# Retention feeding a routed expert layer: the first list made a little later, two guessed loads made one, and sixteen zero scatters made three

## The chip, the cores and the metric

The kernel runs on one core of a Trainium2 chip. The metric is device microseconds from the start to the end of one execution. The core has five instruction streams: TensorE (PE in the profile; PEld is its weight load), VectorE (DVE), ScalarE (ACT), GpSimd (POOL) and SyncE (SP). SP here issues the plain loads, and POOL issues the indirect DMAs, which write rows to places given by a list of row numbers.

## The reference

Two stages follow each other. The first is a retention layer (a linear attention with a decaying state) over 4 sequences, 8 heads, 768 steps and 64 features. The second sends each of the 3072 resulting rows to one of 8 experts, a two-layer network of 512 by 1024 by 512.

```python
for t in range(S):
    state = gamma[None, :, None, None] * state + np.einsum('bhd,bhe->bhde', k[:, :, t], v[:, :, t])
    y[:, :, t] = scale * np.einsum('bhd,bhde->bhe', q[:, :, t], state)
...
logits = x @ w_gate + modality_bias[modality_id]
e_idx = np.argmax(logits, axis=1)
...
for e in range(E):
    mask = e_idx == e
    h = np.maximum(x[mask] @ w1[e], 0.0)
    out[mask] = gate_w[mask, None] * (h @ w2[e])
```

`gate_w` is the softmax probability of the chosen expert. All inputs are float32.

## The kernel before, in words

**Retention.** The 3072 rows are 24 blocks of 128, numbered n. For each block the kernel loads keys and queries (`kq`) and keys and values by token (`kv`), 512 KB each. The first nine blocks go in a "whole" form (scores L277, state L299, output L313 and L319), the later ones in "quarters" (all at L267). A block's output is copied transposed (`yT`, L325), multiplied with a matrix that also holds the gate (L379), and becomes rows of x (`xs`, DVE L387 and ACT L401) and logits (`lh`).

**Routing.** Three blocks are a group. For a group, `route_a` finds each row's expert and adds to the counts `cnt`; `ranks` turns the counts into the fill of 96 candidate slots of 256 rows (matmul `pc` L619, then a key per slot); `route_b` gives each row its place (matmul `rk` L456 to L463); `gates` fills the gate into the rows; `scatter` (L485, POOL) writes the group's three blocks of rows to their places in `x_dram`. After groups 1, 2, 4, 5 and 6 `early_a` and `early_b` make a short list of two full slots (matmuls `pk` L641 and `pt` L692, list `lst` L696). A list is two slots, so ten jobs "e"; a final list brings two jobs "s" and some remainders of 32 rows. After group 0 a guess is made: the expert with most rows so far (`lst_g`). Its weights are loaded before the first list is known.

**A job** is 256 rows through one expert. SP reads slot and expert from the list into registers (TENSOR_LOAD L958), loads two row tiles `xg` of 128 rows (L810), then the expert's w1 and w2 as four tiles `raw1` and four `raw2` of 512 KB (L778, or L780 where the load is skipped if the expert is the one already there). `cut` splits a weight tile in two parts, `hi` by ACT (L784) and `lo` by DVE (L786). The rows are transposed by PE (`xp_e` L829) and split too (`xTh` by ACT L798, `xTl` by DVE L799). Then `first_slot` (L844) makes h with three products for each pair of parts, `second` (L859) makes o, ACT scales it (L871) and POOL scatters it to the output (L872).

**Order.** PE, ACT, DVE and SP work in the order in which the program writes their instructions; POOL's order is found by a scheduler. The program advances in steps. At each step one function of the list `todo` is taken (`tick`), and retention goes on to its next `yield`. Before the first job there are only retention and routing; once the first list is there, the row loads and weight loads of the first job are issued, `AHEAD` steps are counted down while retention goes on, the first two `cut`s of w1 and the transposes (`flip_x`) fall in steps on the way, and then the job begins. In a job of some 14 steps, every third step takes one step of retention.

**Zero rows.** The last slots of each expert are not full. After the final list `pad_a`, `pad_b` and `pad_c` compute the places behind each expert's last row, and 16 indirect DMAs (two for each expert, 128 rows of 2056 bytes each, `pad_c` L545) write zero rows there. Places that need no zeros get a number out of bounds. The row loads of the last three jobs wait for these scatters.

Of the kernel before, what the change touches and what calls it, by code (L numbers as in the profile page):

```python
# [7 lines left out]
F32 = mybir.dt.float32  # L8
F32R = mybir.dt.float32r
BF16 = mybir.dt.bfloat16  # L10
# [24 lines left out]
NTAIL = 2  # L35
NUNIT = 144

AHEAD = 6

WHOLE = 9  # L40
EMPTY = 2 * NCAND
# [12 lines left out]
def kernel(  # L54
# [23 lines left out]
    def bank(name):  # L78
        return ps.tile([P, 512], F32, tag="bank", name=name)
# [10 lines left out]
    lent = {("kq", n): f"hi2{n - 4}" for n in range(4, 8)}  # L90
    lent.update({("kv", n): f"lo2{n - 3}" for n in range(3, 7)})

    def room(kind, n, bufs):
        shape, name = [P, 2, DM], f"{kind}_{n}"
        if (kind, n) in lent:
            return me.tile(shape, F32, tag=lent[kind, n], name=name)
        return ld.tile(shape, F32, tag=kind, name=name, bufs=bufs)

    def load_kq(n, parts=1):
# [71 lines left out]
    def zero_rows(nm):  # L171
        zer = wk.tile([P, ROW], F32, tag="xs", name=nm, bufs=6)
        nc.gpsimd.memset(zer, 0.0)
        nc.gpsimd.memset(zer.bitcast(I32)[:, DM : DM + 1], NT)
        return zer
# [318 lines left out]
        scattered.setdefault(gr, []).append(getattr(ins, "ins", ins))  # L494


    def pad_a():
        tot = bank("tot")[:, :NE]
        nc.tensor.matmul(tot, ones, cnt[NGRP], start=True, stop=True)
        shape = [P, NE, 2]  # L500
        at = cp.tile(shape, F32, name="pad_at")
        row = cp.tile([P, 2], F32, name="pad_row")
        nc.gpsimd.iota(
            row, [[P, 2]], base=0, channel_multiplier=1, allow_small_or_imprecise_dtypes=True
        )

        num = cp.tile([P, NE], F32, name="pad_num")
        nc.vector.tensor_copy(num, tot)
        numi = cp.tile([P, NE], I32, name="pad_numi")
        nc.vector.tensor_copy(numi, num)  # L510
        lasti = cp.tile([P, NE], I32, name="pad_lasti")
        nc.vector.tensor_scalar(lasti, numi, SLOT - 1, None, op0=ALU.bitwise_and)
        last = cp.tile([P, NE], F32, name="pad_last")
        nc.vector.tensor_copy(last, lasti)
        none = cp.tile([P, NE], F32, name="pad_none")
        nc.vector.tensor_scalar(none, last, 0.0, float(SLOT), op0=ALU.is_equal, op1=ALU.mult)
        nc.vector.tensor_tensor(last, last, none, op=ALU.add)
        nc.vector.tensor_tensor(
            at, last.unsqueeze(2).to_broadcast(shape), row.unsqueeze(1).to_broadcast(shape),
            op=ALU.add,  # L520
        )
        over = cp.tile(shape, F32, name="pad_over")
        nc.vector.tensor_scalar(
            over, at, float(SLOT), float(2 * ZROW), op0=ALU.is_ge, op1=ALU.mult
        )
        nc.vector.scalar_tensor_tensor(
            num, iota3[:, 0], float(NT), num, op0=ALU.mult, op1=ALU.add
        )
        mid["pad"] = (row, num, over)

    def pad_b():
        row, num, over = mid.pop("pad")
        shape = [P, NE, 2]
        nc.vector.tensor_tensor(
            over, over, num.unsqueeze(2).to_broadcast(shape), op=ALU.add
        )
        mid["zero"] = zero_rows("zer2")
        pad = mid["pad"] = cp.tile(shape, I32, name="pad_i")
        nc.vector.tensor_tensor(
            pad, over, row.unsqueeze(1).to_broadcast(shape), op=ALU.add  # L540
        )

    def pad_c(e):
        for h in range(2):
            ins = nc.gpsimd.indirect_dma_start(  # L545
                out=x_dram[:, :],
                out_offset=bass.IndirectOffsetOnAxis(ap=mid["pad"][:, e, h : h + 1], axis=0),
                in_=mid["zero"],
                in_offset=None,
                bounds_check=ZROW - 1,  # L550
                oob_is_err=False,
            )
            disjoint(ins, "x_rows")


    off_c = cnd[:, 0:1]
# [245 lines left out]
    def load_rows(tag, at, full=None):  # L802
        xg = []
        assert sum(len(scattered.get(gr, [])) for gr in range(NGRP if full is None else full + 1)) == (
            NN if full is None else (full + 1) * GRP
        )
        for hh, r in enumerate(at):
            t = me.tile([P, ROW], F32, tag=f"xg{hh}", name=f"xg{hh}_{tag}", bufs=2)
            r = r() if callable(r) else r
            ins = nc.sync.dma_start(t, x_dram[bass.ds(r * P, P), :])  # L810
# [358 lines left out]
    def everything():  # L1169
# [171 lines left out]
```

## Time and profile before

| | us |
|---|---|
| runs of the kernel before | 431.11, 432.29, 435.65 |
| their median | 432.29 |
| the profiled execution, its own time | 429.24 |
| its span, as the trace has it | 427.2 |
| PE busy in the span | 403.8 (95%) |
| DVE, ACT, POOL busy | 247.5, 207.7, 103.1 |

The span runs from the first to the last instruction that the trace shows; 2.04 us of the profiled execution's time lie around it. The profiled execution is 3.05 us faster than the median. "PEclk" or the granted clock is the share of TensorE's full clock that it was allowed in a stretch. A row of a window view gives the window, its length, and the busy time and count of PE, PEld, DVE, ACT and POOL, then PE's clock, the DMA share and GB/s. A row of the timeline gives start, duration, engine, line, operation, what it writes from what, shapes and count, and in square brackets how long the engine was idle before it and what ended that. A row of the wait view gives who waited for what, the total, how often, and the longest.

### The profile page before, as it was taken

The numbers are of one execution on the slowest core, as the hardware profiler recorded it, in microseconds if no ns is written. First come the engines' busy times: TensorE is split into PE (matmuls) and PEld (weight loads), VectorE is DVE, ScalarE is ACT, GpSimd is POOL, SyncE is SP. The second block draws the span as 40 slices with busy tenths as digits, with TensorE's granted clock in tenths as the row PEclk, the third lists the DMA queues.
The fourth block names the chain that finished last, engine by engine and source line by source line (L and its number), as shares of the span: only waits on it lengthen the run. The fifth ranks groups of instructions, "written<-read, shape, count | busy, mean of one in ns | idle before, by whom it ended". The sixth has DMA issues, their size and how long they took to land.

```text
span 427.2 us, 12026 instructions
## 1 busy us (share of the span) xinstructions
PE 403.8 (95%) x4596; PEld 352.8 (83%) x4596; DVE 247.5 (58%) x590; ACT 207.7 (49%) x420; POOL 103.1 (24%) x130
## 2 busy tenths in 40 slices
PE   4998869999999999999999999999999999999994
PEld 3887749988968977988898998989899898967863
DVE  1775537855726674756754765768565574634700
ACT  1233346754627444655645564655465563636511
POOL 2424401233033114112510210130486100002001
PEclk9998979999999999999999999999999999999998
DMA  8999748877787955137760213762253898999001
GB/s 289 398 405 371 270 143 263 297 265 252 255 294 261 302 209 187 50 125 254 241 224 28 94 58 123 269 201 76 67 174 130 310 337 280 383 387 345 27 0 45
DMA packets 30891, 92.79 MB, mean 217 GB/s; under 512 B 5550, under 2 KB 5678, under 8 KB 30832
## 3 DMA queue, kind: packets, MB, share of 16 engines
q1 hardware_dynamic: 25360, 77.83, 52.8%
q0 software_dynamic: 5184, 13.67, 8.6%
q8 instruction: 37, 0.61, 0.6%
q10 hardware_dynamic: 288, 0.50, 0.3%
q14 instruction: 22, 0.18, 0.1%
HBM read 94.84 MB, written 17.21 MB: 262 GB/s over the span
## 4 chain that ended last, share of the span: by engine, by line
PE 54%; issue 17%; DMA 5%; DVE 3%; POOL 3%; ACT 2%; POOLq 1%; SPq 0%; ACTq 0%
PE o_e L859 20%; PE h_e L844 20%; PE x L379 4%; PE st L267 3%; PE sc L267 3%; PE y L267 2%; DVE lo_e L786 2%; PE xp_e L829 2%; ACT hi_e L784 1%; DMA kv<-in_qkv_dram 1%; POOL out_dram L872 1%; POOL x_dram L545 1%; DMA x_dram<-zer,pad_i 1%; DMA xg_e<-x_dram 1%; DMA wa_u<-in_w_dram 1%
## 5 line engine op out<-in xcount | busy, mean ns | idle before, releaser
L786 DVE TENSOR_TENSOR lo_e<-raw,hi_e 128x1024 fp32r<-128x1024 f32 x80 | 99.8, 1248 | 83.9 <-ACT hi_e L784 75.9
L844 PE MATMUL h_e<-xTh,hi_e 128*128 128x256 f32 x320 | 91.8, 287 | 0.0
L844 PE MATMUL h_e<-xTl,hi_e 128*128 128x256 f32 x320 | 90.3, 282 | 0.0
L844 PE MATMUL h_e<-xTh,lo_e 128*128 128x256 f32 x320 | 90.3, 282 | 0.0
L784 ACT CAST hi_e<-raw 128x1024 fp32r<-128x1024 f32 x80 | 83.7, 1047 | 3.9 <-DMA raw<-in_w_dram 3.9
L859 PE MATMUL o_e<-hi_e,hTh 128*128 128x512 f32 x160 | 66.3, 414 | 0.0
L859 PE MATMUL o_e<-lo_e,hTh 128*128 128x512 f32 x160 | 63.1, 395 | 0.0
L859 PE MATMUL o_e<-hi_e,hTl 128*128 128x512 f32 x160 | 63.1, 394 | 0.0
L844 PEld LDWEIGHTS h_e<-xTh,hi_e 128*128 128x128 f32 x320 | 60.7, 190 | 0.7
L844 PEld LDWEIGHTS h_e<-xTh,lo_e 128*128 128x128 f32 x320 | 60.6, 190 | 0.3
L844 PEld LDWEIGHTS h_e<-xTl,hi_e 128*128 128x128 f32 x320 | 60.7, 190 | 0.0
L1032 POOL TENSOR_TENSOR vd<-kv,cst 128x512 f32<-128x512 f32 x24 | 27.2, 1133 | 96.7 <-PE y L267 38.7
L793 ACT ACTIVATE hTh<-h_e 128x256 fp32r<-128x256 f32 x80 | 30.7, 386 | 34.0 <-PE h_e L844 29.9
L872 POOL DMA_INDIRECT out_dram<-o_e,xg_e x20 | 20.6, 1032 | 110.2 <-ACT o_e L871 90.4
L401 ACT ACTIVATE xs<-x,cst 128x64 f32<-128x64 f32 x96 | 22.2, 314 | 43.7 <-DVE lh L387 25.1
L794 DVE SCALAR_TENSOR_TENSOR hTl<-h_e,hTh 128x256 fp32r<-128x256 f32 x80 | 33.1, 419 | 16.5 <-ACT hTh L793 14.8
L485 POOL DMA_INDIRECT x_dram<-xs,pos x24 | 26.9, 1119 | 44.9 <-DVE a L212 17.2
L859 PEld LDWEIGHTS o_e<-lo_e,hTh 128*128 128x128 f32 x160 | 30.1, 188 | 7.1
L859 PEld LDWEIGHTS o_e<-hi_e,hTh 128*128 128x128 f32 x160 | 30.1, 188 | 6.1
L859 PEld LDWEIGHTS o_e<-hi_e,hTl 128*128 128x128 f32 x160 | 30.2, 189 | 5.5
L871 ACT ACTIVATE o_e<-o_e,xg_e 128x512 f32<-128x512 f32 x20 | 13.8, 690 | 40.8 <-issue 23.9
L379 PE MATMUL x<-wgt,yT 128*128 128x144 f32 x192 | 30.7, 304 | 1.8 <-issue 1.8
(193 smaller groups left out, 677.8 us busy)
## 6 DMA issues: line engine op xcount, KB each, us to landing
raw<-in_w_dram SPq DMA_DIRECT2D x104, 512.0 KB
kv<-in_qkv_dram SPq DMA_DIRECT2D x24, 512.0 KB
kq<-in_qkv_dram SPq DMA_DIRECT2D x23, 512.0 KB
xg_e<-x_dram SPq DMA_DIRECT2D x20, 257.0 KB
wa_u<-in_w_dram SPq DMA_DIRECT2D x8, 512.0 KB
wb_u<-in_w_dram SPq DMA_DIRECT2D x16, 256.0 KB
xg_s<-x_dram SPq DMA_DIRECT2D x4, 257.0 KB
x_dram<-xs,pos POOLq DMA_INDIRECT x24
```

The costliest lines, as they stand in the source:

```text
L267: nc.tensor.matmul(out_, l, r, start=start, stop=True, skip_group_check=True)
L379: nc.tensor.matmul(px[:, g], yT[:, 2 * u + g], wgt[:, 2 * u + g], start=(g == 0), stop=(g == 1), skip_group_check=True,)
L401: nc.scalar.activation(x[:, i], px[:, i // 2, rows(i % 2)], AF.Copy, scale=gain[:, c, 4 * u + i : 4 * u + i + 1],)
L485: ins = nc.gpsimd.indirect_dma_start(out=x_dram[:, :], out_offset=bass.IndirectOffsetOnAxis(ap=pos[:, i : i + 1], axis=0), in_=xs, in_offs ...
L784: nc.scalar.copy(hi, raws[m][i])
L786: nc.vector.tensor_tensor(lo, raws[m][i], hi.bitcast(F32), op=ALU.subtract)
L793: nc.scalar.activation(hi, src, AF.Relu)
L794: nc.vector.scalar_tensor_tensor(lo, src, 0.0, hi.bitcast(F32), op0=ALU.max, op1=ALU.subtract)
L844: nc.tensor.matmul(ph, s["w1"][f // 2][wi][:, o : o + P], s["xT"][kc // 2][a][:, kc % 2, :], start=(n == 0), stop=(n == 3 * KC - 1),)
L859: nc.tensor.matmul(po, hT[f][a][:, hh * P : (hh + 1) * P], s["w2"][f // 2][wi][:, (f % 2) * DM : (f % 2 + 1) * DM], start=(n == 0), stop=( ...
L872: ins = nc.gpsimd.indirect_dma_start(out=out[:, :], out_offset=bass.IndirectOffsetOnAxis(ap=xg.bitcast(I32)[:, DM : DM + 1], axis=0), in_= ...
L1032: ins = nc.gpsimd.tensor_tensor(vds[n], vv, by[:, n % NCH].unsqueeze(2).to_broadcast([P, H, D]), op=ALU.mult)
```

## The change

1. **The guess.** Only the guessed expert's w1 is loaded ahead of the first list. The first job's w2 is loaded without condition once the list is there. `AHEAD` goes from 6 to 4 and the cuts and the flip are renumbered.
2. **The first list.** In group 1, gates, places and the scatters of the rows (`first_b`) come ahead of the candidate sizes; the list (`d`) is made two ticks later than before. Both row registers are loaded before both row loads. In group 4 a step of waiting is put in, so everything from there on in that group is a step later.
3. **The zero scatters.** The four rotating `kq` tiles become parts of one tile `four`, which after the last `kq` is set to zero by POOL and serves as source. Places are computed for runs of 8 rows (16,448 bytes for one row number) and single rows: two indirect DMAs write runs (experts 0 to 3 and 4 to 7), one writes single rows. `pad_a` (DVE) now comes before the three small matmuls of the new `pad_m`, and `pad_b` has 17 DVE operations.

The diff, cut to its core:

```diff
-AHEAD = 6
+RUN = 8
+AHEAD = 4
...
+    four = ld.tile([P, max(4 * QW, RUN * ROW)], F32, name="four", bufs=1)
+    fours = [four[:, i * QW : (i + 1) * QW] for i in range(4)]
+    free = [i for i in range(NN) if ("kq", i) not in lent]
...
+        if kind == "kq":
+            return fours[free.index(n) % 4].rearrange("p (a b) -> p a b", a=2)
...
     def pad_a():
-        tot = bank("tot")[:, :NE]
-        nc.tensor.matmul(tot, ones, cnt[NGRP], start=True, stop=True)
...
+    def pad_m():
+        spread, base, j = mid.pop("pad")
+        tot = bank("tot")
+        for i in range(3):
+            nc.tensor.matmul(
+                tot[:, i : i + 1], spread[:, i], ones[:, 0:1], start=True, stop=True
+            )
+        mid["zero"] = zer = four[:, : RUN * ROW].rearrange("p (r c) -> p r c", c=ROW)
+        nc.gpsimd.memset(zer, 0.0)
+        nc.gpsimd.memset(zer.bitcast(I32)[:, :, DM : DM + 1], NT)
+        mid["pad"] = (tot[:, :3], base, j)
...
-    def pad_c(e):
-        for h in range(2):
-            ins = nc.gpsimd.indirect_dma_start(
-                out=x_dram[:, :],
-                out_offset=bass.IndirectOffsetOnAxis(ap=mid["pad"][:, e, h : h + 1], axis=0),
-                in_=mid["zero"],
...
+    def pad_c(i):
+        n = RUN if i else 1
+        zer = mid["zero"].rearrange("p r c -> p (r c)")
+        ins = nc.gpsimd.indirect_dma_start(
+            out=x_dram[:, :].rearrange("(n r) c -> n (r c)", r=n),
+            out_offset=bass.IndirectOffsetOnAxis(ap=mid["pad"][:, i : i + 1], axis=0),
+            in_=zer[:, : n * ROW],
+            in_offset=None,
+            bounds_check=ZROW // n - 1,
+            oob_is_err=False,
+        )
...
     def unit(tag, e, at):
-        wa = [ld.tile([P, QW], F32, tag="kq", name=f"wa{i}_{tag}", bufs=4) for i in range(4)]
+        wa = fours
...
-        s["at"] = [lambda h=h: reg(lst, at + h * n + i, EMPTY) for h in range(s["nh"])]
+        s["at"] = [reg(lst, at + h * n + i, EMPTY) for h in range(s["nh"])]
         if j is jobs[0]:
             rows_in(s)
-        else:
-            s["at"] = [r() for r in s["at"]]
...
+        def first_b():
+            gates(gr)
+            route_b(gr)
+            rows_out()
+            ranks(gr, EVENTS[gr], mid["first"])
+
         def c():
-            if gr not in EVENTS or gr == min(EVENTS):
+            if gr not in EVENTS:
                 rows_out()
...
-            todo.extend([a1, b, c, d])
+            todo.extend([a1, wait, first_b, wait, c, d])
...
         elif gr < 5:
-            todo.extend([a, a1, b, c])
+            todo.extend([a, a1, wait, b, c])
...
-                todo.extend([wait, final_m, wait, final_b, pad_a, wait, pad_b, wait])
-                todo.extend([lambda e=e: pad_c(e) for e in range(NE)])
+                todo.extend([wait, final_m, wait, final_b, pad_a, wait, pad_m, wait, pad_b, wait])
+                todo.extend([lambda i=i: pad_c(i) for i in (1, 2, 0)])
...
                 raw(guess, 1)
-                raw(guess, 2)
...
                     raw(job, 1, guess)
-                    raw(job, 2, guess)
+                    raw(job, 2)
...
-                if ahead in (3, 4):
-                    cut(job, 1, 4 - ahead)
-                if ahead == 2:
+                if ahead in (2, 3):
+                    cut(job, 1, 3 - ahead)
+                if ahead == 1:
                     flip_x(job)
```

Three places show what this does to the order. The first is PE around the first list's last step, the `pt` matmuls; `x` is tokens_out, `y_7` the output of block 7, `sc` and `st` scores and state. Before:

```order
L641 MATMUL pk_763<-dg,onef 96x96
L379 MATMUL x_0_778<-wgt,yT_698 128x144 x2
L379 MATMUL x_1_783<-wgt,yT_698 128x144 x2
L692 LDWEIGHTS vals
L692 MATMUL pt_794<-ohs,vals 1x2
L692 LDWEIGHTS vals
L692 MATMUL pt_794<-ohs,vals 1x2
L692 LDWEIGHTS vals
L692 MATMUL pt_794<-ohs,vals 1x2
L313 MATMUL y_7_845<-kq_145,s_7_640 64x128
```

The same matmuls on PE, now:

```order
L328 MATMUL y_7_773<-a_674,vd_618 64x128 x4
L670 MATMUL pk_795<-dg,onef 96x96
L308 MATMUL st_620<-vd_690,kv_228 64x64 x8
L276 MATMUL sc_817<-four 64x64 x16
L344 MATMUL st_834<-s_9_813,cst 64x64 x8
L721 LDWEIGHTS vals
L721 MATMUL pt_846<-ohs,vals 1x2
L721 LDWEIGHTS vals
L721 MATMUL pt_846<-ohs,vals 1x2
L388 MATMUL x_0_901<-wgt,yT_790 128x144 x2
```

`pk` stands behind `y_7` instead of ahead of it, and `pt` behind block 7's state, block 9's scores and the hand-over of the state (L344, before L335). The matmuls in between are the ones that stood behind `pt` before. Line numbers of the new kernel are some 9 to 29 higher for the same code.

The second place is ACT from the first job's first weight split to its rows' split (`hi_e` is a weight tile's high part, `s_9` the state of block 9, `xs` rows of x). Before:

```order
L262 COPY s_9_906<-st_897 128x256
L784 CAST hi_e_908<-raw_102 128x1024
L401 ACTIVATE xs_914<-x_1_921,cst 128x64 x4
L262 COPY s_9_938<-st_897 128x256
L784 CAST hi_e_940<-raw_103 128x1024
L325 COPY yT_962<-y_8_944 128x256
L325 COPY yT_962<-y_8_945 128x256
L798 CAST xTh_974<-xp_e_969 128x512
L798 CAST xTh_983<-xp_e_978 128x512
```

The same stretch of ACT now:

```order
L271 COPY s_9_843<-st_834 128x256
L410 ACTIVATE xs_899<-x_1_906,cst 128x64 x4
L271 COPY s_9_923<-st_834 128x256
L813 CAST hi_e_925<-raw_102 128x1024
L334 COPY yT_947<-y_8_929 128x256
L334 COPY yT_947<-y_8_930 128x256
L813 CAST hi_e_953<-raw_103 128x1024
L271 COPY s_10_975<-st_834 128x256
L827 CAST xTh_998<-xp_e_993 128x512
L827 CAST xTh_1007<-xp_e_1002 128x512
```

Both weight splits moved behind copies that retention needs: the first behind block 8's `xs` and block 9's second state copy, the second behind `yT`. On PE the eight transposes `xp_e`, which stood ahead of all of block 9's quarters work, now stand in the middle of it.

The third place is POOL at the end (`out_dram` are the rows of finished jobs). Before:

```order
L485 DMA x_dram<-xs_4333,pos_4576 24704x514
L872 DMA out_dram<-o_e_4730,xg_e_4299 3072x512
L872 DMA out_dram<-o_e_4799,xg_e_4301 3072x512
L545 DMA x_dram<-zer_4988,pad_i 24704x514 x9
L872 DMA out_dram<-o_e_5074,xg_e_4700 3072x512
L545 DMA x_dram<-zer_4988,pad_i 24704x514 x7
L872 DMA out_dram<-o_e_5142,xg_e_4702 3072x512
```

The same stretch of POOL now:

```order
L494 DMA x_dram<-xs_4310,pos_4553 24704x514
L900 DMA out_dram<-o_e_4707,xg_e_4276 3072x512
L900 DMA out_dram<-o_e_4776,xg_e_4278 3072x512
L574 DMA x_dram<-four,pad_i 3088x4112
L900 DMA out_dram<-o_e_5065,xg_e_4677 3072x512
L574 DMA x_dram<-four,pad_i 3088x4112
L900 DMA out_dram<-o_e_5124,xg_e_4679 3072x512
L574 DMA x_dram<-four,pad_i 24704x514
L900 DMA out_dram<-o_e_5362,xg_e_5011 3072x512
```

Nine and seven zero scatters stood ahead of the two halves of a job's output; now one run scatter stands ahead of each, and the scatter of single rows behind both.

More of the change, by code (lines that the diff above doesn't have):

```diff
@@ L497, in pad_a @@
     def pad_a():
-        tot = bank("tot")[:, :NE]
-        nc.tensor.matmul(tot, ones, cnt[NGRP], start=True, stop=True)
[L500 to L504, printed above, removed]
-        )
-        num = cp.tile([P, NE], F32, name="pad_num")
-        nc.vector.tensor_copy(num, tot)
-        numi = cp.tile([P, NE], I32, name="pad_numi")
@@ L510, in pad_a @@
[L510 to L541, printed above, removed]
@@ L543, in pad_c @@
-    def pad_c(e):
-        for h in range(2):
-            ins = nc.gpsimd.indirect_dma_start(
-                out=x_dram[:, :],
-                out_offset=bass.IndirectOffsetOnAxis(ap=mid["pad"][:, e, h : h + 1], axis=0),
-                in_=mid["zero"],
[L549 to L553, printed above, removed]
+        spread = cp.tile([P, 3, P], BF16, name="pad_cnt")
+        for to, n in ((spread[:, 0], 16), (spread[:, 1:].rearrange("p d c -> p (d c)"), 32)):
+            nc.vector.tensor_copy(
+                to.rearrange("p (e j) -> p e j", j=n),
+                cnt[NGRP].unsqueeze(2).to_broadcast([P, NE, n]),
+            )
@@ new lines, in pad_a @@
+        num = cp.tile([P, 3], I32, name="pad_num")
+        nc.gpsimd.iota(num[:, 0:1], [[0, 1]], base=0, channel_multiplier=1)
+        nc.gpsimd.iota(num[:, 1:], [[P, 2]], base=0, channel_multiplier=1)
+        ji = cp.tile([P, 3], I32, name="pad_ji")
+        nc.vector.tensor_scalar(ji[:, 0:1], num[:, 0:1], 15, None, op0=ALU.bitwise_and)
+        nc.vector.tensor_scalar(ji[:, 1:], num[:, 1:], 31, None, op0=ALU.bitwise_and)
+        j = cp.tile([P, 3], F32, name="pad_j")
+        nc.vector.tensor_copy(j, ji)
@@ new lines, in pad_a @@
+        base = cp.tile([P, 3], F32, name="pad_base")
+        nc.vector.tensor_copy(base, num)
+        nc.vector.tensor_tensor(base, base, j, op=ALU.subtract)
+        nc.vector.tensor_scalar(base[:, 0:1], base[:, 0:1], NT / 16.0, None, op0=ALU.mult)
+        nc.vector.tensor_scalar(base[:, 1:], base[:, 1:], NT / 32.0, None, op0=ALU.mult)
+        mid["pad"] = (spread, base, j)
+    def pad_m():
[9 more added lines that the diff above has]
+        mid["pad"] = (tot[:, :3], base, j)
@@ new lines, in pad_b @@
+    def pad_b():
+        tot, base, j = mid.pop("pad")
+        num = cp.tile([P, 3], F32, name="pad_tot")
+        nc.vector.tensor_copy(num, tot)
+        left = cp.tile([P, 3], F32, name="pad_left")
+        nc.vector.tensor_scalar(left, num, -1.0, float(NT), op0=ALU.mult, op1=ALU.add)
+        lefti = cp.tile([P, 3], I32, name="pad_lefti")
+        nc.vector.tensor_copy(lefti, left)
+        ones_i = cp.tile([P, 3], I32, name="pad_ones_i")
+        nc.vector.tensor_scalar(ones_i, lefti, RUN - 1, None, op0=ALU.bitwise_and)
+        one = cp.tile([P, 3], F32, name="pad_one")
+        nc.vector.tensor_copy(one, ones_i)
+        nc.vector.tensor_scalar(lefti, lefti, SLOT - 1, None, op0=ALU.bitwise_and)
+        nc.vector.tensor_copy(left, lefti)
+        nc.vector.tensor_tensor(base, base, num, op=ALU.add)
+        nc.vector.tensor_tensor(base[:, 1:], base[:, 1:], one[:, 1:], op=ALU.add)
+        for t in (left, base):
+            if t is left:
+                nc.vector.tensor_tensor(t[:, 1:], t[:, 1:], one[:, 1:], op=ALU.subtract)
+            nc.vector.tensor_scalar(t[:, 1:], t[:, 1:], 1.0 / RUN, None, op0=ALU.mult)
+        nc.vector.tensor_copy(left[:, 0:1], one[:, 0:1])
+        nc.vector.tensor_tensor(base, base, j, op=ALU.add)
+        over = cp.tile([P, 3], F32, name="pad_over")
+        nc.vector.tensor_tensor(over, j, left, op=ALU.is_ge)
+        nc.vector.tensor_scalar(over, over, float(2 * ZROW), None, op0=ALU.mult)
+        at = mid["pad"] = cp.tile([P, 3], I32, name="pad_i")
+        nc.vector.tensor_tensor(at, over, base, op=ALU.add)
@@ L556 @@
+    def pad_c(i):
[8 more added lines that the diff above has]
+            oob_is_err=False,
+        )
+        disjoint(ins, "x_rows")
     off_c = cnd[:, 0:1]
@@ L808, in load_rows @@
             t = me.tile([P, ROW], F32, tag=f"xg{hh}", name=f"xg{hh}_{tag}", bufs=2)
-            r = r() if callable(r) else r
             ins = nc.sync.dma_start(t, x_dram[bass.ds(r * P, P), :])
```

## The prediction

> **What bounds the kernel now.** I read the head of the page first, then PE's waits in two parts, then the stretch with the longest of them in windows of 2 us.
>
> ```profile
> span 427.2 us, 12026 instructions
> PE 403.8 (95%) x4596; PEld 352.8 (83%) x4596; DVE 247.5 (58%) x590; ACT 207.7 (49%) x420; POOL 103.1 (24%) x130
> ```
>
> PE is idle for 23.4 us in all. Its waits before 66 us, and then after:
>
> ```profile
> PE xp_e L829 <- DMA xg_e<-x_dram: 2.1, 2, 1.1
> PE st L267 <- ACT s L262: 2.1, 1, 2.1
> PE sc L267 <- issue: 1.2, 3, 0.5
> ...
> PE pt L692 <- DVE ohs L682: 0.7, 1, 0.7
> PE pc L619 <- DVE crep L614: 0.4, 1, 0.4
> PE xp_e L829 <- DMA xg_e<-x_dram: 0.4, 1, 0.4
> ```
>
> Only the first job's start has waits worth a change: 4.2 us for `xg_e` and `s`. In the windows the third field from the end is the granted clock, the field behind the window's length PE's busy time:
>
> ```profile
> 36.00:38.00 2.00, 0.42 (x8) 0.07 (x4) 0.00 (x0) 0.62 (x4) 1.70 (x2) 1.00 1.06 406
> 38.00:40.00 2.00, 1.71 (x7) 1.71 (x8) 0.48 (x2) 0.89 (x3) 1.22 (x3) 0.62 0.98 373
> 40.00:42.00 2.00, 2.00 (x18) 1.72 (x17) 1.36 (x8) 1.12 (x5) 0.00 (x0) 0.53 1.13 337
> ...
> 56.00:58.00 2.00, 0.33 (x3) 0.14 (x1) 0.00 (x0) 0.83 (x1) 0.00 (x0) 1.00 0.52 169
> 58.00:60.00 2.00, 1.34 (x7) 0.94 (x7) 1.75 (x3) 0.21 (x1) 0.00 (x0) 0.74 0.00 0
> 60.00:62.00 2.00, 0.07 (x4) 0.08 (x7) 0.87 (x5) 1.32 (x6) 0.00 (x0) 0.50 0.35 92
> 62.00:64.00 2.00, 2.00 (x76) 2.00 (x80) 1.15 (x2) 2.00 (x5) 0.21 (x1) 0.50 0.99 397
> ```
>
> From 56 to 62 PE is busy for 1.74 of 6 us: 4.26 idle. And the clock falls to half, so the work that follows runs at half speed until 65.7 (the x rows below start there and take their usual time). That stretch, in the timeline:
>
> ```profile
> 47.01 0.21 PE L692 MATMUL pt<-ohs,vals 96*1 96x2 bf16 x3 [0.25 <-issue]
> 48.89 0.14 DVE L696 TENSOR_TENSOR lst<-pt,base_e 1x6 int32<-1x6 f32 x1
> 49.36 0.97 POOL L485 DMA_INDIRECT x_dram<-xs,pos  x1 [0.30 <-issue]
> 52.09 0.69 PE L335 MATMUL st<-s,cst 128*64 128x64 f32 x16
> 54.15 1.92 SPq L810 DMA_DIRECT2D xg_e<-x_dram  x2
> 54.93 1.09 PE L319 MATMUL y<-a,vd 128*64 128x128 f32 x16
> 57.06 0.30 PE L829 MATMUL xp_e<-cst,xg_e 128*128 128x128 f32 x1 [1.03 <-DMA xg_e<-x_dram]
> 57.07 3.09 SPq L780 DMA_DIRECT2D raw<-in_w_dram  x8
> 58.47 1.34 PE L829 MATMUL xp_e<-cst,xg_e 128*128 128x128 f32 x7 [1.11 <-DMA xg_e<-x_dram]
> 65.77 1.25 PE L379 MATMUL x<-wgt,yT 128*128 128x144 f32 x8
> 66.76 0.37 PE L844 MATMUL h_e<-xTh,hi_e 128*128 128x256 f32 x1
> ```
>
> and in the chain of waits:
>
> ```profile
> 57.17 1.05 ACT hi_e L784
> ...
> 59.39 0.68 DVE a L212
> ...
> 61.61 0.27 ACT s L262
> ```
>
> The list is there at 49, but the rows' loads wait on SP until 54.15 for group 1's scatters, whose last was issued at 49.36. PE stands before the transposes `xp_e`. Beside that ACT stands at its first `hi_e`, which waits for the guarded w1 loads of 57.07 (the guess holds here, they move nothing). DVE's `lo_e` follows, then `a`, then `xs`, `s`, and so block 9's state, which PE waits for until 61.92. Two waits, one cause: everything stands behind the first list's loads.
>
> **The change, part by part.**
>
> *The first list.* Up to the hand-over (L335) PE does the same work before `pt` as before, so `pt` comes at 52.8 and ends at 53.0 instead of 47.2, with the three "issue" waits of 1.2 us kept. The list I put 0.3 later, 53.3, as DVE has nothing long there. The scatters are now ahead of the sizes, so the list comes last, and SP reads two registers first. One such read costs about 1.0 (the second row load ended at 54.15 + 1.92 = 56.07, and the guarded loads behind the next read start at 57.07). So the loads go out at 55.3 and 55.65, and the rows land 2.9 later as before (54.15 to 57.06): 58.2 and 58.5.
>
> PE meanwhile: `x`, state and output took from 52.70 to 56.02, now 53.0 to 56.1 or so. In before the whole of block 9's quarters ran from 61.92 to 65.77 at half the clock, 3.85 us, so 1.9 at full clock. Half of it now stands ahead of `xp_e`: 57.1. PE idles 1.1 us to 58.2. The eight transposes end by 59.4 (the row has 1.34 for seven at a clock well below full, so 0.9 from the second tile's landing), the other half at 60.3, and `x` (1.2) at 61.5. Block 9's state no longer waits for the weight split, since ACT's `hi_e` has moved behind `xs` and `s`: that wait of 2.1 goes, and next late is the row load.
>
> ACT's chain to the first product:
>
> ```profile
> 62.68 0.68 ACT L325 COPY yT<-y 128x256 f32<-128x256 f32 x2
> 63.21 1.13 ACT L798 CAST xTh<-xp_e 128x512 fp32r<-128x512 f32 x2
> 63.99 1.28 DVE L799 TENSOR_TENSOR xTl<-xp_e,xTh 128x512 fp32r<-128x512 f32 x2
> 74.36 1.04 ACT L784 CAST hi_e<-raw 128x1024 fp32r<-128x1024 f32 x1
> ```
>
> The guarded w1 loads pass at about 57.05 and the first `hi_e` ends at 58.15; `yT` follows (0.7), the second `hi_e` (1.0) to 59.9, a state copy (0.3), then `xTh` at 60.2 to 61.3 and the first `xTl` at 61.75. PE and this chain meet: the first `h_e` at about 61.7 against 66.76. Gain 5.1. Without the issue waits it would be 6.2.
>
> Whether the idle time costs the clock too is open. The windows from 36 to 40 have 1.87 us without PE work around 38, and the clock is at half from there to 42: one such gap was enough. The three issue waits (1.2 us together, around 50) were followed by none. The new 1.1 us lies nearer to those, so I take no loss; if it costs, it costs what it did there: 0.38 and 0.47 of two windows of 2 us, 1.7.
>
> The Trainium skill, page "TensorE: Matmul & The Clock Gate", section "Part 1: The HAM clock gate (the "warmup" mystery)", says that the clock is halved after an idle window of about 3.4 us. By that rule the new gap could cost nothing, rival 1 below would have no chance, and the sum would stay as it is. The gap around 38 is about half that long and did cost the clock; the measurement decides, and rival 1 keeps its chance.
>
> *w2 no longer guessed.* Four loads of 512 KB leave the early queue and come unguarded behind the list, at 58 to 59; at the 397 GB/s of the row from 62 to 64 they take 5.3 us: landed at 63 to 64. Their first use is ACT's split, at 74.36 before and so about 69.3 now. The cover is 5 us. What pays for it: block 12's `kq` and `kv` and the second job's w1 stand behind these 2.1 MB on SP and in the DMA engines. I take nothing, since the DMA engines stood idle from 58 to 60 (0.00), where w2 now goes; the other end is all of it, 5.3.
>
> *Group 4 a step later.* It is meant for `pc` and `pt`, which waited 0.4 and 0.7 there. Bounds 0 and 1.1 gained; I take 0.5, because a step later only helps if DVE has caught up.
>
> *The zero scatters.* They now cost three DMAs and an address chain.
>
> ```profile
> L545 POOL DMA_INDIRECT x_dram<-zer,pad_i x16 | 18.3, 1145 | 14.5 <-issue 14.2 <-DMA out_dram<-o_e,xg_e 0.3
> ...
> L173 POOL MEMSET zer<- 128x514 f32 x2 | 1.1, 543 | 0.0
> ...
> 310.86 1.23 DVE L786 TENSOR_TENSOR lo_e<-raw,hi_e 128x1024 fp32r<-128x1024 f32 x1 [4.65 <-ACT o_e L871]
> 311.22 1.72 POOL L545 DMA_INDIRECT x_dram<-zer,pad_i  x1 [0.30 <-issue]
> 316.57 0.98 POOL L872 DMA_INDIRECT out_dram<-o_e,xg_e  x1 [0.30 <-ACT o_e L871]
> ...
> 317.85 3.91 DMA x_dram<-zer,pad_i
> ...
> 328.72 2.44 SPq L810 DMA_DIRECT2D xg_e<-x_dram  x2
> ```
>
> POOL loses 13 x 1.145 = 14.9 us, but POOL is idle for three quarters of the span, and PE waits only 0.4 for the rows loaded at 328.72. So at most that 0.4 is gained. Against it: two more small matmuls on PE (0.2 each with their weights, by the pt row, about 0.4). Net 0. `pad_b`'s 17 small DVE operations (an estimate of 0.2 each, above the 0.14 of the one that makes `lst`: 3.4) fall into the gap of 4.65 that DVE had before `lo_e` at 310.86. The memset is eight times as long as 543 ns, 4.3 us, on an idle POOL.
>
> *Sum.* 5.1 + 0.5 + 0 = 5.6 off the profiled execution's 429.24: 423.6. On the scale of the median, which is 3.05 higher: 432.29 - 5.6 = 426.7.
>
> **The rivals.**
>
> 1. *The clock falls once more.* The gap before `xp_e` is a little longer or falls badly into a window. Gain 3.4 + 0.5 = 3.9: 428.4. For it: the gap of 1.87 around 38. Against: 1.1 is shorter. Chance 0.14.
> 2. *The gain is taken back by the queue.* With w2 behind the list, `kq`, `kv` and the second job's w1 come late by up to 5.3, and a later block or the second job waits: anywhere up to no gain, 432.3. For it: 0.99 and 397 GB/s from 62 on show that the queue is full then. Against: the empty 58 to 60. Chance 0.16. That the run scatters eat part of the gain (below): another 0.03.
> 3. *Slower: a run scatter holds POOL.* One run scatter names 128 places of 16,448 bytes, eight times a row. If POOL's time for it is T, the order is run, output, run, output, singles. DVE's gap begins at 306.2, so the places are ready at 309.6. Two runs, two outputs, the singles (1.3 each with POOL's 0.30 between) and the landing of 3.91 follow: the tenth job's rows can be loaded at 309.6 + 3 x 1.3 + 3.9 + 2T = 317.4 + 2T. They are needed at about 328.4, as their load went out at 328.72 with 0.4 of waiting. It decides from T = 5.5. With eight times 0.98, 7.8 us, 4.6 is lost and the change still gains 1.0; with eight times 1.72, 13.8 us, 16.6 is lost: 429.24 - 5.6 + 16.6 = 440.2, on the median's scale 443.3. For it: nothing in this trace has 16 KB to a row number. Against: the cost of one on POOL would have to grow with its bytes; the sixteen rows have one size and cannot say. Chance 0.09.
>
> That the change does not do what it says: the order shows the moves, and that the guess holds in this input shows in the loads at 57.07; nothing more to that.
>
> **How the numbers follow.** The forecast has 0.58, with a range of its own from 425.0 (issue waits gone and all 1.1 of group 4: 7.3) to 428.2 (row loads 1 us later, nothing from group 4: 4.1). A measurement of this kernel tells about 1% from no change, 4.3 us, so faster means below 427.97. Of the forecast 0.06 lies at or above that. Faster: 0.52. Within 1%: 0.06 + 0.14 + 0.16 + 0.03 = 0.39. Slower: 0.09. The range goes from 424.0 to 431.0: it leaves out the slower case and the worst part of the second rival, some 0.17, and reaches 1.0 below the forecast's own for the 0.4 of `xp_e` and for the spread of the runs.
>
> **What would show it.** In the new profile: the first `h_e` near 61.7; the wait of `st` for `s` gone; `xg_e` issued at 55 to 56, right behind the list; one idle stretch of about 1 us before `xp_e` and a clock of 1.00 from 58 on. The row loads of the tenth job go out well before 328 minus the gain. Wrong would be: a clock of 0.5 behind `xp_e` (rival 1), waits of `sc`, `st` or `h_e` for `kq`, `kv` or `raw` after 62 (rival 2), run scatters of more than 5 us on POOL with `xp_e` waiting at 325 (rival 3).

## The result, and the profile after

The changed kernel took 420.21 us in the median of six runs (418.65 to 420.89), the kernel before 433.15 in the median of six (431.11 to 435.65). The ratio is 0.970, with an interval of 0.966 to 0.974: 12.9 us faster, where 5.6 was forecast. The sign was right; the time lies 3.8 below the lower end of the range.

The first thing to see is that the difference has two parts. The profiled executions, 429.24 before and 420.01 after, lie 9.2 apart. The other 3.7 is the distance of before's runs from its own profiled execution (433.15 against 429.24); the changed kernel has no such distance (420.21 against 420.01). The 420.01 is one of the six runs, the 429.24 is none of before's and lies below all of them. Head of the page, and PE's waits of the changed kernel, before 66 us and then after:

```profile
span 418.2 us, 12000 instructions
PE 400.0 (96%) x4598; PEld 349.8 (84%) x4598; DVE 251.7 (60%) x605; ACT 207.3 (50%) x420; POOL 91.6 (22%) x118
...
PE x L388 <- issue: 1.4, 1, 1.4
PE sc L276 <- issue: 1.3, 3, 0.5
PE st L308 <- POOL vd L1058: 0.9, 1, 0.9
PE x L388 <- ACT yT L334: 0.7, 1, 0.7
...
PE y L276 <- issue: 1.2, 3, 0.4
PE st L276 <- issue: 0.4, 1, 0.4
```

No wait for `xg_e`, for `s`, for `pc` or for `pt` is left. The start of the first job in the timeline of the changed kernel:

```profile
36.44 0.76 PE L388 MATMUL x<-wgt,yT 128*128 128x144 f32 x4 [1.38 <-issue]
37.87 0.76 PE L388 MATMUL x<-wgt,yT 128*128 128x144 f32 x4 [0.68 <-ACT yT L334]
49.64 1.12 PE L344 MATMUL st<-s,cst 128*64 128x64 f32 x16
50.69 0.21 PE L721 MATMUL pt<-ohs,vals 96*1 96x2 bf16 x3
50.95 0.15 DVE L725 TENSOR_TENSOR lst<-pt,base_e 1x6 int32<-1x6 f32 x1 [1.43 <-PE pt L721]
52.59 0.90 SPq L838 DMA_DIRECT2D xg_e<-x_dram  x2
56.19 1.09 PE L857 MATMUL xp_e<-cst,xg_e 128*128 128x128 f32 x8
59.29 0.37 PE L872 MATMUL h_e<-xTh,hi_e 128*128 128x256 f32 x1
```

and its windows, in the form of those before:

```profile
38.00:40.00 2.00, 2.00 (x26) 1.73 (x28) 1.35 (x7) 1.15 (x6) 0.54 (x1) 1.00 0.96 386
40.00:42.00 2.00, 2.00 (x44) 1.93 (x42) 1.83 (x7) 1.19 (x4) 1.04 (x1) 1.00 0.33 107
...
46.00:48.00 2.00, 1.59 (x39) 1.32 (x38) 1.90 (x9) 1.10 (x6) 1.54 (x2) 1.00 0.55 199
48.00:50.00 2.00, 1.10 (x15) 0.85 (x16) 1.52 (x1) 0.74 (x3) 1.47 (x2) 0.88 0.54 195
50.00:52.00 2.00, 2.00 (x24) 1.85 (x21) 0.97 (x4) 0.37 (x1) 0.00 (x0) 0.50 0.90 164
52.00:54.00 2.00, 2.00 (x37) 1.65 (x36) 0.98 (x4) 0.60 (x3) 0.00 (x0) 0.77 0.50 148
```

The first `h_e` starts at 59.29 against 66.76: 7.5 earlier. `pt` runs at 50.69, 2.1 ahead of the 52.8 that I worked out; the row loads go out 1.6 behind the list (I had 2.0), nothing of SP's waiting for scatters is left, and PE is busy without a gap from 50 to 66.

Not all of the 7.5 is the change's doing. Here is the way to it in the two profiles, first before, then after: the first `x`, and the `x` and `sc` around 38.

```profile
15.37 1.25 PE L379 MATMUL x<-wgt,yT 128*128 128x144 f32 x8
38.30 2.15 PE L379 MATMUL x<-wgt,yT 128*128 128x144 f32 x8 [1.77 <-issue]
40.38 1.87 PE L277 MATMUL sc<-kq 64*128 64x128 f32 x16
```

```profile
14.22 1.25 PE L388 MATMUL x<-wgt,yT 128*128 128x144 f32 x8
38.56 1.16 PE L286 MATMUL sc<-kq 64*128 64x128 f32 x16
```

The first `x` comes 1.15 earlier, and the changed kernel is still 1.16 ahead at the `x` of 31.72 (32.88 before). Up to there the two kernels do the same retention work. The first `sc` takes 2.08 us in both and later ones 1.16; which matmul is the first at full speed differs from one execution to the next. In all the profiles of this document the first `x` stands between 13.93 and 15.73, and a further profile of the kernel before (b_same, below) has it at 14.19 instead of 15.37. So the 1.15 is no more than one kernel's own spread, chance and not the change, and profiles below are compared with their first `x` beside them.

The rest of the 9.2 appears at group 4 and at the tenth job: following the scaling of each job's output (ACT) through both traces, the distance is 6.6 at the first output, 7.4 to 7.5 at the next three, 8.5 to 8.7 from the fifth on, behind group 4's step, and 9.2 from the eighteenth on, behind the wait of 0.4 for the rows loaded at 328.72 in before.

At the end POOL has the three scatters, here the memset and the two run scatters, from POOL's timeline:

```profile
243.12 3.53 POOL L537 MEMSET four<- 128x4112 f32 x1 [4.47 <-PE y L276]
...
300.80 0.98 POOL L574 DMA_INDIRECT x_dram<-four,pad_i  x1 [16.05 <-issue]
302.08 0.98 POOL L900 DMA_INDIRECT out_dram<-o_e,xg_e  x1 [0.30 <-issue]
303.37 0.98 POOL L574 DMA_INDIRECT x_dram<-four,pad_i  x1 [0.30 <-issue]
```

A scatter with 128 numbers for runs of 16,448 bytes holds POOL for 0.98 us, as one for rows of 2056 bytes does. Numbers that need no zeros are out of bounds, so fewer than 128 runs are written; how many, the profile does not say. T was 0.98, and rival 3, which needed 5.5, is gone.

### The profile page after: what moved, and what is told of

Same layout as the page of the kernel before. It is cut to its first block, busy times and chain, and to the rows that moved or that the text cites. A ratio compares the mean times of both kernels' runs of the same rounds, so it can differ in the third digit from the quotient of the medians.

```text
span 418.2 us, 12000 instructions
## 1 busy us (share of the span) xinstructions
PE 400.0 (96%) x4598; PEld 349.8 (84%) x4598; DVE 251.7 (60%) x605; ACT 207.3 (50%) x420; POOL 91.6 (22%) x118
## 4 chain that ended last, share of the span: by engine, by line
PE 82%; issue 8%; DMA 4%; DVE 3%; POOL 1%; POOLq 0%; ACT 0%; SPq 0%; ACTq 0%
PE h_e L872 28%; PE o_e L887 27%; PE x L388 6%; PE sc L276 3%; PE st L276 3%; PE h_s L872 3%; PE y L276 2%; PE xp_e L857 2%; DMA four<-in_w_dram 2%; PE sc L286 2%; PE y L328 2%; DMA cst<-in_consts_dram 1%; DVE a L296 1%; PE st L308 1%; PE y L322 1%
## 5 line engine op out<-in xcount | busy, mean ns | idle before, releaser
L1058 POOL TENSOR_TENSOR vd<-kv,cst 128x512 f32<-128x512 f32 x24 | 28.2, 1174 | 99.6 <-DMA kv<-in_qkv_dram 40.4
```

The lines of the kernel that those rows point to most:

```text
L1058: ins = nc.gpsimd.tensor_tensor(vds[n], vv, by[:, n % NCH].unsqueeze(2).to_broadcast([P, H, D]), op=ALU.mult)
```

## Experiments

Each group of kernels ran on one chip beside before, on five chips in all; the chip of the first comparison is not on record. The first four kernels make one part of the change each.

**The w2 load alone.**

```diff
                 raw(guess, 1)
-                raw(guess, 2)
...
-                    raw(job, 2, guess)
+                    raw(job, 2)
```

> The kernel before, with only the w2 loads changed: none for the guess, the first job's w2 loaded without condition behind its list. Theory A (what counts is that the row loads and the weight split no longer hold up PE): those waits stay, so the first h_e stays at 66 to 67 and the time within 1 us of before. Theory B (2.1 MB less on the DMA queues before 45 us is what brings the start forward): first h_e 2 us or more earlier and the time 2 to 4 us lower.

422.98 against 424.12, ratio 0.998 (0.996 to 0.999): 1.1 faster. The first `h_e` came at 65.57. In b_g4 on the same chip, with w2 guessed, it came at 65.67; counted from the first `x` (15.56 and 14.83) it is 0.8 earlier without the guess, and the row loads go out 4.7 us behind the list instead of 6.1. Theory B asked for 2 to 4 us; it falls. The 1.1 is more than theory A's "within 1" by a hair, and its interval (0.3 to 1.5) holds both.

**The first list's order alone.** `AHEAD`, cuts, flip, `first_b` and the registers as in the change; w2 still guessed.

```diff
-            todo.extend([a1, b, c, d])
+            todo.extend([a1, wait, first_b, wait, c, d])
```

> The kernel before, with only the order of the first list changed: gates, places and scatters ahead of the sizes, list two ticks later, AHEAD 4, cuts and flip renumbered, both registers read before both row loads; w2 still guessed. Theory A: this is the whole gain of the start, first h_e at 59 to 61 and 6 to 8 us lower than before. Theory B: less than half of it, first h_e at 63 or later, 2 to 4 us lower. Theory C (the clock: before's runs lose more to the halved clock than its profiled execution did, and every kernel without the idle stretch is spared that): the runs' median falls by 3 us more than the profile's first h_e moves.

419.62 against 424.12, ratio 0.990 (0.988 to 0.992): 4.5 faster, the largest part. The first `h_e` came at 61.94, between the two theories' limits. Theory C, by which the runs would fall by 3 more than the profile, finds nothing here; but before's runs were not slow on this chip, so it is not tested where it was needed.

**The step in group 4 alone.**

```diff
-            todo.extend([a, a1, b, c])
+            todo.extend([a, a1, wait, b, c])
```

> The kernel before, with only the waiting step in group 4. All theories: the waits of pc (0.4) and pt (0.7) go, 1.1 us lower; the first h_e where it was. If a later wait takes it up again, 0.

422.75 against 424.12, ratio 0.997 (0.996 to 0.998): 1.4 faster, as expected of the 1.1 in waits.

**The zero scatters alone** (the diff's part 3).

> The kernel before, with only the zero scatters changed (one tile for the four kq buffers, three indirect DMAs). Theory A: between 0 and 0.6 us lower, since only the last wait for the rows (0.4) goes. Theory D (the sixteen scatters cost more in the timed runs than in the profiled one): 2 to 4 us lower.

422.87 against 424.12, ratio 0.997 (0.996 to 0.999): 1.25 faster, above theory A's 0.6, though its interval reaches down to 0.3; theory D falls.

The surprise was before itself: 424.1 here and 433 in the first comparison. So both kernels ran again on another chip, with their profiles.

> The kernel before itself, for its profile on this chip. If the waits named issue (x 1.8, sc 1.2) belong to one chip or session, they are gone here and the first h_e comes 1 to 3 us earlier than 66.8; if they belong to the program, they are there again.

> The changed kernel itself beside it. Theory A (parts add up): before's 424.1 less 4.5 (list), 0.9 (w2), 1.3 (group 4) and 1.2 (zero scatters) as measured alone, so 416 or so. Theory E (list and w2 need each other: with w2 guessed the scatters of group 1 take over 6 us to land and the row loads still wait for them): 1 to 3 us below that sum, 413 to 415.

b_same took 424.07, a_same 418.25, and the before beside them 424.92; a_same's ratio is 0.984 (0.981 to 0.987), 6.7 us. The issue waits on PE are gone from both profiles. Yet b_same's first `h_e` came at 66.88, not 1 to 3 earlier. Its list is there 2.5 earlier than before's (46.35 against 48.89), but its row loads go out only 0.5 earlier (53.67 against 54.15), and its clock then stays at half for 10.2 us (56.3 to 66.5, worked out from the clock's shares in the windows) instead of 6.8. PE's waits in b_same from 40 to 75 us:

```profile
PE xp_e L829 <- DMA xg_e<-x_dram: 5.5, 2, 4.6
PE st L267 <- ACT s L262: 1.8, 1, 1.8
PE pc L619 <- DVE crep L614: 1.5, 1, 1.5
```

And in a_same, with the chain of waits from 40 to 60 us behind them:

```profile
PE xp_e L857 <- DMA xg_e<-x_dram: 4.2, 2, 3.3
PE st L344 <- ACT s L271: 1.1, 1, 1.1
...
45.72 6.22 DMA x_dram<-xs,pos
...
52.51 4.06 DMA xg_e<-x_dram
```

Here the row loads do wait for group 1's scatters again: the last is issued at 45.72 and has landed 6.22 us later, while the list is there at 48. So "the list comes last" holds in the first comparison only, where PE's issue waits push the list to 50.95. The first `h_e` of a_same came at 62.13, 4.75 ahead of b_same (first `x` at 13.96 and 14.19). That looks like my 61.7 and 5.1, but those were for a kernel with the issue waits; for one without I had 6.2. The parts measured alone sum to 4.5 + 1.1 + 1.4 + 1.25 = 8.3, and the whole gives 6.7 at most, so they seem to overlap (the parts ran on another chip), and theory E's "more than the sum" falls.

**List and w2 together.**

> The kernel before with the first list's new order and the w2 load moved, without the step in group 4 and the zero scatters. Theory A: 424.1 - 4.5 - 0.9 = 418.7, and xp_e still waits for xg_e. Theory E: 416 to 417.5; xp_e waits for nothing, the row loads go out within 2 us of the list, h_e starts before 60.

419.65 against 424.92, ratio 0.988 (0.985 to 0.991): 5.3 faster, near theory A's sum, and `xp_e` still waits 3.3 for `xg_e` in the first job. Theory E's 416 to 417.5 falls here too.

**The weight split a step earlier**, in the changed kernel:

```diff
                     ahead = AHEAD
+                    cut(job, 1, 0)
...
-                if ahead in (2, 3):
-                    cut(job, 1, 3 - ahead)
-                if ahead == 1:
+                if ahead == 3:
+                    cut(job, 1, 1)
+                if ahead == 2:
                     flip_x(job)
```

> The changed kernel with the first two weight splits and the transposes a step earlier, as they stood relative to the list before. My prediction's step (the split ahead of xs and s holds up block 9's state): PE waits 1 to 2 us for s or xg_e again, the clock falls again, 1.5 to 4 us slower than the changed kernel. Rival: with row loads out so early the place does not matter, within 0.5 us.

421.71, ratio 0.992 (0.989 to 0.996), 3.5 slower than a_same beside it. ACT's rows, a_cut, and behind them the same copy in a_same:

```profile
55.31 1.05 ACT L813 CAST hi_e<-raw 128x1024 fp32r<-128x1024 f32 x1 [6.56 <-DMA raw<-in_w_dram]
58.83 0.93 ACT L410 ACTIVATE xs<-x,cst 128x64 f32<-128x64 f32 x4 [2.47 <-DVE lh L396]
59.63 0.39 ACT L271 COPY s<-st 128x256 f32<-128x256 f32 x1
...
50.26 0.39 ACT L271 COPY s<-st 128x256 f32<-128x256 f32 x1
```

The state's copy ends at 60.0 behind a cast that itself waited 6.56 us (DVE's `lo_e`, `a` and `lh` and ACT's `xs` stand between them), and PE waits 1.9 for it. In a_same that copy stands at 50.26. By the medians the step of order is worth half of the whole change; between the two profiles the first `h_e` is 2.8 later (64.95 against 62.13), of which 0.7 is there at the first `x` (14.65 against 13.96). This is the chain that the prediction had read out of before. (The transposes move with the split in this kernel; they wait 4.5 in all for `xg_e`, against 4.2 in a_same.)

**The changed kernel on further chips.**

> The changed kernel once more, to see whether its distance to before belongs to the chip. Theory F (the 3% of the first comparison is a chip on which PE has its issue waits and before is above 430): where these waits are missing the ratio is again 0.983 to 0.986; where they are there, 0.975 or less.

> The kernel before again, for one more profile of it. Theory F (a chip with issue waits on PE makes before slower than 430): with such waits in the profile, above 429; without them, 423 to 425.

> The changed kernel again. Theory F: with issue waits on PE the ratio is 0.975 or less, without them 0.983 to 0.986.

> The changed kernel on one more chip. Theory F: ratio 0.975 or less if PE has issue waits there, else 0.983 to 0.987.

a_same2: 417.88 against 424.08, ratio 0.985 (0.982 to 0.988). a_same3: 418.63 against 424.05, 0.987 (0.984 to 0.989). a_same4: 419.63 against 424.42, 0.988 (0.984 to 0.991). b_same2 gave 424.38. With a_same that is 4.8 to 6.7 us on four chips, all without issue waits. That half of theory F holds nearly: 0.987 and 0.988 lie a hair above its 0.986 and 0.987. Its other half was not met again, since no further chip showed these waits.

**Work that nobody reads in place of the idle time.** In before, 32 transposes of the identity ahead of the first job's transposes and 14 behind; in the changed kernel 24 ahead. 

```diff
+    def warm(n):
+        pb = bank("warm")
+        for _ in range(n):
+            nc.tensor.transpose(pb[:, :P], ident, ident)
```

> The kernel before with added work on PE that nobody reads: 32 transposes of the identity ahead of the first job's transposes and 14 behind them, some 6 us at full clock, in the time in which PE waits for the row loads and for block 9's state. If the halved clock behind the idle stretch has its price beside the wait itself, the clock stays at 1.00 from 52 to 66 and the time falls by 2.5 to 4 us although PE does more. If only the waits count, no gain, or a loss of up to 2.

> The changed kernel with 24 such transposes (3.1 us at full clock) ahead of the first job's transposes, where PE waited 3.3 us for the row loads on this kind of chip. Clock theory: the clock stays up or falls for less, 1.5 to 3 us faster than the changed kernel. Otherwise 0 to 1 slower.

> The changed kernel with 24 unread transposes ahead of the first job's, in more rounds. Clock theory: 0.5 to 2 us faster than the changed kernel where PE waits for the row loads; where it has issue waits and no such wait, 2 to 3 us slower.

b_warm took 423.23 against 424.08, ratio 0.998 (0.997 to 1.000): 0.9 faster with more work, less than the 2.5 expected. a_warm took 417.09 (416.62 to 418.51) where a_same2 beside it took 417.88 (417.25 to 419.35), less than the 1.5 expected, and a_warm2 416.99 (416.15 to 417.97) where a_same3 took 418.63 (417.39 to 419.23). Windows of a_same2, then of a_warm, same chip:

```profile
54.00:56.00 2.00, 0.00 (x0) 0.00 (x0) 0.00 (x0) 0.23 (x1) 0.00 (x0) 1.00 0.60 166
56.00:58.00 2.00, 1.10 (x8) 0.89 (x8) 1.15 (x1) 2.00 (x4) 0.00 (x0) 1.00 0.27 102
58.00:60.00 2.00, 2.00 (x66) 1.80 (x64) 1.73 (x3) 1.56 (x4) 0.00 (x0) 0.53 0.66 219
60.00:62.00 2.00, 2.00 (x14) 1.97 (x11) 1.89 (x5) 0.86 (x2) 0.00 (x0) 0.62 0.85 270
```

```profile
54.00:56.00 2.00, 1.83 (x16) 1.43 (x13) 0.00 (x0) 0.61 (x1) 0.00 (x0) 1.00 0.68 209
56.00:58.00 2.00, 1.41 (x39) 1.24 (x39) 1.27 (x2) 2.00 (x5) 0.00 (x0) 1.00 0.03 9
58.00:60.00 2.00, 1.91 (x57) 1.73 (x46) 2.00 (x3) 1.93 (x5) 0.00 (x0) 1.00 0.87 293
60.00:62.00 2.00, 2.00 (x19) 2.00 (x18) 1.93 (x7) 0.41 (x3) 0.00 (x0) 1.00 0.91 287
```

The clock stays whole, and the first job's first output is scaled at 84.9 instead of 86.7. Of these 1.83 us, 0.67 is there at the first `x` (14.39 against 15.06), which leaves 1.16. The other pair seems to say the opposite, 86.41 in a_warm2 against 85.71 in a_same3, but there the first `x` came 1.76 later (15.73 against 13.97), so without that the output is 1.06 earlier. So the halved clock has a price of its own, 1.1 to 1.2 us in the profiles and 0.8 to 1.6 in the medians, whose ranges overlap. a_warm2 has the lowest median of all that ran, but where PE does not wait for the rows, as in the first comparison, its 2.8 us of added work would lie on the path; that was not tried.

**Real work in place of the idle time.** `AHEAD` 5 instead of 4.

> The changed kernel with one more step of retention ahead of the first job (AHEAD 5): real work instead of the wait, the transposes stand behind x of block 8 and the first product behind half of block 10's quarters. If the row loads' landing is what PE waits for, 3 to 5 us faster than the changed kernel, as the wait and most of the half clock go. If the lists of later groups or the weights are next late, 0 to 2 faster.

419.09 against a_same2's 417.88: slower, and both expectations fall. One row of ACT and one wait of PE in it:

```profile
56.69 1.04 ACT L813 CAST hi_e<-raw 128x1024 fp32r<-128x1024 f32 x1 [3.65 <-DMA raw<-in_w_dram]
57.65 0.37 ACT L271 COPY s<-st 128x256 f32<-128x256 f32 x1
...
PE st L276 <- issue: 3.9, 1, 3.9
```

The cast stands ahead of the state's copy again, and the state waits for the weights as in a_cut: the profile calls it "issue", but the `st` that waits starts at 58.11, right behind the end of that copy at 58.02.

**The changed kernel less one part.** w2 guessed again (the first diff turned round), and without the step in group 4.

> The changed kernel with w2 guessed and loaded early again. If the early 2.1 MB delay the landing of group 1's scatters (six us from issue, for which the row loads wait on SP), 0.8 to 2 us slower than the changed kernel, with the row loads going out 1 to 2 us later. My prediction's sum had nothing for it: within 0.5.

> The changed kernel without the waiting step in group 4. The waits of pc (0.4) and pt (0.7) come back: 1.0 to 1.4 us slower than the changed kernel. My prediction had 0.5.

a_w2 took 419.57 and a_g4 419.75, a_same4 beside them 419.63 (all within each other's range): neither the 0.8 expected of a_w2 nor the 1.0 of a_g4 shows in the runs. In the profiles there is something: in a_w2 the last scatter takes longer to land, here ahead of that of a_same4:

```profile
46.98 8.08 DMA x_dram<-xs,pos
...
45.66 6.48 DMA x_dram<-xs,pos
```

The row loads go out 6.0 us behind the list instead of 4.1. But no time is lost by it in the profiles: the first job's first output is scaled 0.8 later than in a_same4 (88.14 against 87.34), and the first `x` is already 1.4 later (15.30 against 13.93). In a_g4 the waits of `pc` (0.4) and `pt` (0.7) are back, and the last output comes at 412.68 against 411.13, with the first `x` at the same place (13.95 and 13.93).

## Why the prediction was wrong

**The first list, the term of 5.1.** It measured 7.5 in the first pair of profiles and 4.75 in the second. The step that failed in the first is "Up to the hand-over (L335) PE does the same work before `pt` as before, so `pt` comes at 52.8". The same work, yes, but not in the same time: `pt` came at 50.69. That is 2.1 of the 2.4 that were missing, and more than half of it, 1.15, is chance: it stood at the first `x`, ahead of all that the change touches. The rest came up around 40, where before ran at a clock of 0.62 and 0.53 and the changed kernel at 1.00: before's `x` and `sc` took 2.15 and 1.87 us there, and behind them, at `y` (42.17 against 39.65), the distance is 2.5. Some 0.4 of that went again at the hand-over, which took 1.12 us at the changed kernel's own halved clock instead of 0.69. The prediction had this clock and its price of 1.7 in front of it and took it to stay; the wait of 1.77 ahead of it is missing from the lines of waits that it shows. Around 37 the changed kernel has as much idle time (1.38 and 0.68, against 1.77 before), so less idle time is not what spared the clock; what did is not shown.

The reading of the chain held: the weight split stood ahead of the state's copy (a_cut), and with it out of the way PE's wait of 2.1 for `s` behind the transposes is gone. The first `h_e` foreseen at 61.7 and met at 62.13 in a_same is luck, since the issue waits that the sum kept were not there and the row loads, which it had at 2.0 behind the list, came at 4.0.

**A landing that I left out.** "The scatters are now ahead of the sizes, so the list comes last" is wrong on the four further chips: SP waits 2.5 to 3.0 us there for scatters that take 6.2 to 7.0 us to land. The two errors met: in a_same the row loads went out 51.95 - 47.99 = 4.0 behind the list instead of 2.0, but the list itself was there at 48 instead of 53.3, as PE had no issue waits and no halved clock ahead of it and its first `x` came 1.4 earlier than in before. For the same reason "Without the issue waits it would be 6.2" is wrong: where they were gone it was 4.75, with the row loads waiting for the scatters.

**The clock (rival 1).** It fell in every profile of both kernels. In the first of the changed kernel it fell behind three issue waits (0.38, 0.45, 0.44), which I had put down as free; on the others behind the gap before `xp_e`, as rival 1 had it, but that gap was 3.0 to 3.3 us and not 1.1. By the rule that the prediction weighed (the Trainium skill, page "TensorE: Matmul & The Clock Gate", section "Part 1: The HAM clock gate (the "warmup" mystery)": an idle window of about 3.4 us) the first of these could not have happened; the trace disagrees with it at 1.27 us, as it did at 1.87.

**w2 and the queue (rival 2).** Nothing came late: behind 62 us PE waits for nothing in a_same, a_same2, a_same3 and a_same4, and only "issue" in the first profile. Taking nothing was right for the changed kernel (a_w2); on the kernel before, the move alone gained 1.1. That fits a shorter landing of the scatters (row loads 4.7 behind the list in b_w2, 6.1 in b_g4), but it is one pair of profiles.

**Group 4, 0.5; zero scatters, 0.** In the first profiles 1.1 (the upper bound) and 0.6. For the second I charged 0.4 for two small matmuls that show nowhere as lost time. DVE, the memset and POOL were covered as said. Rival 3 fell with T = 0.98.

**The sum against the median.** The last step, "on the scale of the median, which is 3.05 higher", assumes that both kernels' runs lie as far from their profiles. They did not: 3.9 before, 0.2 after. This 3.7 is the largest single miss, and its cause stays open. The 429.24 is none of the runs that it was set beside. The first comparison is also the only one in which before took over 430 us; on four further chips the same two kernels differ by 4.8 to 6.7, around the 5.6 of the sum, though that sum was made for a kernel with issue waits. Whether issue waits, the clock or something else of that chip or session made before's runs slow and not the changed kernel's could not be tried, since it was not met again.

## What to carry to other kernels

On an engine that works in program order, look at what a long wait stands ahead of, not only at what waits: a weight split that waited for its load held up a 0.4 us copy, which held up the whole retention, and moving it one step was worth about half of the change. When work on a path moves earlier, check again what lands last; here it was a scatter's landing, not its issue. Before two profiles are set side by side, look at how far apart they are ahead of all that was changed; here it was up to 1.8 us. And do not carry a forecast from one profiled execution to a median of few runs as a constant.

## What was not expected of the hardware

- POOL needs 0.98 us for an indirect DMA with 128 numbers, whether a number stands for 2056 or for 16,448 bytes (some of the latter out of bounds), and 3.53 us for a memset of 128x4112, less than eight times the 543 ns of 128x514.
- The last of three scatters of 128 rows of 2056 bytes has landed 6.2 to 7.0 us after its issue among other loads, and 7.3 (b_list) and 8.1 (a_w2) where another 2.1 MB had been loaded ahead.
- PE's clock was halved behind 1.27 us of idle time spread over three gaps within 2 us (0.38, 0.45, 0.44, after) and behind one gap of 1.77 (before). It was not halved behind 1.17 us spread alike (0.24, 0.49, 0.44, before), nor behind one gap of 1.46 (b_same, ahead of `pc`), nor behind 1.38 and 0.68 (after). So the idle time alone does not tell it; what else counts was not measured. It stayed at half for 3.4 us (after), 6.8 (a_same) or 10.2 (b_same), worked out from the clock's shares in the windows.
- PE's first matmuls run slowly (`sc` 2.08 us against 1.16 later), and how long they do differs between executions: the first `x` starts between 13.93 and 15.73 us in the twenty profiles.
